# VectorE's conversion passes and scale chains: order as written, until all weights are converted

## The chip, the cores and the metric

The kernel runs on one core of a Trainium2 chip. A core has TensorE (PE, with its weight loads shown as PEld), VectorE (DVE), ScalarE (ACT), GpSimd (POOL) and SyncE (SP, which here issues the DMAs). The metric is the device time of one execution in microseconds, lower is better. Each engine takes its instructions strictly in the order of its own queue, and waits at the head of it when an input isn't there.

## The reference, cut to what matters

```python
# 8 batches, 8 heads, 512 local and 32 global tokens, head dim 64
s_ll = where(abs(i - j) <= 32, scale * q_l @ k_l.T, -1e9)      # band of 65 keys
out_l = softmax([scale * q_l @ k_g.T, s_ll]) @ [v_g, v_l]
out_g = softmax(scale * q_g @ [k_g, k_l].T) @ [v_g, v_l]
x = concat(out_g, out_l)  -> [4608, 512]
h = x @ w_in                                                   # [4608, 2048]
g = where(h > 0, h, exp(min(h, 0)) - 1)
out = g @ w_out                                                # [4608, 512]
```

The weights arrive as 64-bit floats, and are turned into 32-bit ones on the chip with integer operations.

## The kernel before, in words

**Two streams of work.** Attention goes through slots (a batch, two pairs of heads, a tile of 128 tokens): scores (L644 adds the mask and takes the row maximum, L647 scales it), the exponential on ACT (L651), the norm (L655, L656, then POOL), transposes on PE (L669), the product with v (L691), and the result into a block xr of 256 tokens with its maximum xm (L703, L705). The FFN goes through 17 such blocks; for each it multiplies by pairs of 128-column tiles of w_in (ffn1, L298), applies the ELU (ACT L307 to L309, DVE L316), and multiplies by w_out (ffn2, L373). Numbers are split in a high and a low half of 16 bits (xh and xl, gh and gl, winh and winl, wouth and woutl), and three products are summed.

**Converting the weights.** w_in and w_out come in 16 units (`unit(m, p)`, 8 pairs of each). A unit loads `raw` by DMA, and then runs in steps: s0 (ACT, then POOL L160), s1a (L164), s1b (L167) and s1c (L171), which put the bits of the 32-bit number together in `cu`, s1d (the maximum: DVE L176 for w_in, ACT for w_out), s2 (`all_max`: a PE transpose L112 and a DVE maximum L113 over all partitions, into `cm`), s3 (a chain of operations on one column, L185, L107, L187, L188, that makes the scale; then ACT L189 writes the high half) and s4 (DVE L192 writes the low half). `tables(group)` makes the scales of a group of pairs in the same way (L208 to L215, `wm_b`, `wm_c`), and POOL multiplies them into `xs` (L476 to L480).

**Splitting a block.** `split_x` does the same with a block of x: L465, `all_max`, L454, L107, L456, L457, then ACT L458 writes xh and DVE L461 writes xl.

**Groups.** While not all weights are there, a block goes through the pairs in groups a (pair 0), b (pair 1), c (2 and 3) and d (4 to 7), and its partial sums go through DRAM (`o`, L381 adds them). Once all are converted (the key "f" is in `tab`), a block goes through all eight pairs at once, with seven products of quarter blocks for eight (L413); sums of weights for that are made by `add_up` (L251 to L266).

**What sets the order.** The program writes the steps with `defer(n, fn)`: the function runs n ticks later, and a tick comes with each slot of attention or stretch of the FFN. The scheduler then sets each engine's queue by its own estimate of when operations can start, and may let an operation overtake others that were written ahead of it. `tc.keep_in_program_order(op)` adds an edge from the instruction written last ahead of `op` on its engine, which takes no semaphore and only sets order: `op` can't come ahead of that instruction. Others can still move around them. In the kernel before, two kinds of operation are held in this way: s1a (L164) and the PE transpose of `all_max` (L112).

## Time and profile before

| | us |
|---|---|
| median of 3 runs | 1017.06 |
| the runs | 1019.08, 1017.06, 1016.84 |
| the profiled execution | 1018.12 |
| its span in the trace | 1016.3 |
| PE busy in the span | 965.1 (95%) |
| DVE busy | 785.8 (77%) |
| ACT busy | 685.9 (67%) |
| POOL busy | 247.0 (24%) |

The profile is one execution. A row of the timeline has the start in microseconds from the beginning of the span, the length, the engine, the line of the kernel, the operation, and the tiles written and read; in brackets stands how long the engine was idle ahead of it, and what released it. A row of the windows has the span and each engine's busy time, then the clock that PE was granted (1.00 is full speed), the share of DMA and its GB/s. Ends of matmuls are modelled. Names in the timeline have no buffer number; where a name here has one (xm_847), it is that of the queues shown below. All 16 units are converted in the first 231 us or so.

### The profile page before, as it was taken

How to read it: one execution, taken by the hardware profiler on the slowest of the kernel's cores; microseconds unless marked ns; L12 is line 12 of the kernel's file. 1: busy time of each engine (PE TensorE's matmuls, PEld its weight loads, DVE VectorE, ACT ScalarE, POOL GpSimd, SP SyncE). 2: the span in 40 equal slices, each digit the busy share in tenths (PEclk: the TensorE clock that was granted, in tenths of full speed). 3: DMA queues.
4: the chain of work that ended last, by engine and by line, in shares of the span. 5: the costliest groups of instructions: out<-in, count | busy, mean ns of one | idle time of the engine just before them, and what ended most of it. 6: DMA issues, size and time to landing. Idle time of an engine off the chain costs nothing.

```text
span 1016.3 us, 21648 instructions
## 1 busy us (share of the span) xinstructions
PE 965.1 (95%) x8128; PEld 775.3 (76%) x8128; DVE 785.8 (77%) x2233; ACT 685.9 (67%) x1561; POOL 247.0 (24%) x442
## 2 busy tenths in 40 slices
PE   6898879989999999999999999999999999999994
PEld 4576546666667788887888888888888888888884
DVE  5789898999986778677777778787787878766663
ACT  4779868767566667676666677667666757677673
POOL 3355654234132112221212122112221211100000
PEclk9799999989999999999999999999999999999998
DMA  7535765641321113001310123012210101000000
GB/s 272 171 121 184 255 215 161 213 152 52 106 77 54 43 69 106 31 17 60 115 52 16 43 79 105 22 37 79 79 43 14 41 22 33 1 22 22 1 22 21
DMA packets 39168, 81.95 MB, mean 81 GB/s; under 512 B 3864, under 2 KB 5912, under 8 KB 39064
## 3 DMA queue, kind: packets, MB, share of 16 engines
q1 hardware_dynamic: 39064, 80.58, 23.7%
q8 instruction: 64, 1.05, 0.4%
q14 instruction: 40, 0.33, 0.1%
HBM read 65.36 MB, written 15.20 MB: 79 GB/s over the span
## 4 chain that ended last, share of the span: by engine, by line
PE 60%; DVE 21%; ACT 13%; issue 3%; POOL 1%; DMA 1%; DVEq 0%; ACTq 0%; POOLq 0%
PE h L298 20%; PE acc L413 9%; PE h L413 5%; PE pa L691 4%; PE pa L669 4%; PE pa L632 4%; ACT p L651 4%; PE pa L298 3%; DVE p L644 3%; PE pa L580 2%; DVE gl L319 2%; PE acc L373 2%; DVE g L316 2%; PE pa L413 2%; ACT g L307 2%
## 5 line engine op out<-in xcount | busy, mean ns | idle before, releaser
L298 PE MATMUL h<-xh,winh 128*128 128x256 f16 x992 | 271.4, 274 | 10.4 <-ACT xh L458 5.8
L298 PE MATMUL h<-xl,winh 128*128 128x256 f16 x992 | 271.1, 273 | 0.1
L298 PE MATMUL h<-xh,winl 128*128 128x256 f16 x992 | 271.2, 273 | 0.0
L298 PEld LDWEIGHTS <-winh 128*128 128x128 f16 x2176 | 211.6, 99 | 49.4 <-issue 20.3
L658 POOL TENSOR_SCALAR p<-p,sm 128x224 f32<-128x224 f32 x256 | 144.1, 580 | 333.5 <-DVE sm L656 191.3
L316 DVE SCALAR_TENSOR_TENSOR g<-g,hs 128x512 f32<-128x512 f32 x136 | 96.2, 707 | 96.2 <-ACT g L309 95.5
L651 ACT ACTIVATE p<-p,m 128x224 f32<-128x224 f32 x256 | 120.2, 473 | 67.1 <-DVE m L647 66.8
L413 PEld LDWEIGHTS <-gh 128*128 128x128 f16 x1456 | 141.8, 98 | 21.0 <-issue 4.8
L298 PEld LDWEIGHTS <-winl 128*128 128x128 f16 x1088 | 106.7, 98 | 13.0 <-issue 0.4
L307 ACT ACTIVATE g<-h,xs 128x512 f32<-128x512 f32 x124 | 84.9, 684 | 45.5 <-PE h L298 45.1
L338 ACT ACTIVATE gh<-gs,xs 128x640 f16<-128x640 f32 x104 | 86.4, 831 | 38.2 <-DVE gs L334 38.2
L319 DVE SCALAR_TENSOR_TENSOR gl<-gs,xs,gh 128x640 f16<-128x640 f32 x104 | 94.2, 905 | 23.1 <-ACT gh L338 22.9
L337 ACT ACTIVATE gh<-g,xs 128x256 f16<-128x256 f32 x104 | 53.3, 512 | 77.1 <-DVE g L316 77.1
L309 ACT ACTIVATE g<-g 128x512 f32<-128x512 f32 x136 | 85.8, 631 | 0.0
L308 ACT ACTIVATE hs<-h,xs 128x512 f32<-128x512 f32 x124 | 84.6, 682 | 0.0
L669 PE MATMUL pa<-ident,p 128*128 128x128 f32 x512 | 79.6, 282 | 3.4 <-POOL p L658 3.4
L413 PEld LDWEIGHTS <-gl 128*128 128x128 f16 x728 | 71.2, 98 | 12.9 <-DVE gl L319 0.5
L413 PE MATMUL acc<-raw,gh 128*128 128x256 f16 x416 | 79.4, 273 | 0.0
L319 DVE SCALAR_TENSOR_TENSOR gl<-g,xs,gh 128x256 f16<-128x256 f32 (+1 forms) x136 | 75.0, 552 | 5.3 <-ACT gh L323 5.1
L644 DVE CUSTOM_DVE_ANT_0 p<-pa,msk 128x224 f32<-128x224 f32 x228 | 76.4, 383 | 2.4 <-PE pa L632 2.2
L672 DVE COPY pt<-pa 128x512 f32<-128x512 f32 x98 | 66.6, 680 | 10.7 <-PE pa L669 10.6
L669 PEld LDWEIGHTS pa<-ident,p 128*128 128x128 f32 x512 | 61.5, 145 | 10.5 <-POOL p L658 6.2
(194 smaller groups left out, 2019.9 us busy)
## 6 DMA issues: line engine op xcount, KB each, us to landing
v<-vT SPq DMA_DIRECT2D x64, 256.0 KB, 2.7
k<-kT SPq DMA_DIRECT2D x32, 448.0 KB, 4.1
out<-o SPq DMA_DIRECT2D x34, 256.0 KB, 2.1
q<-qT SPq DMA_DIRECT2D x32, 256.0 KB, 5.4
raw<-w_in SPq DMA_DIRECT2D x8, 1024.0 KB, 6.2
raw<-w_out SPq DMA_DIRECT2D x8, 1024.0 KB, 5.2
od<-o SPq DMA_DIRECT2D x24, 256.0 KB, 2.5
o<-od SPq DMA_DIRECT2D x24, 256.0 KB, 3.1
```

Source lines behind the costliest of these rows:

```text
L298: nc.tensor.matmul(h[:, j, :], wt[:, c, f], xt[:, c, :], start=k == 0, stop=k == 11)
L307: nc.scalar.activation(g, hf, AF.Relu, scale=sc[:, p:p + 1])
L308: nc.scalar.activation(hs, hf, AF.Copy, scale=sc[:, 2 * NP + 1 + p:2 * NP + 2 + p])
L309: nc.scalar.activation(g, g, AF.Exp, scale=-1.0)
L316: nc.vector.scalar_tensor_tensor(out=g, in0=g, scalar=-1.0, in1=hs, op0=ALU.add, op1=ALU.max)
L319: nc.vector.scalar_tensor_tensor(out=dst, in0=src, scalar=sg, in1=hi, op0=ALU.mult, op1=ALU.subtract)
L338: nc.scalar.activation(gh[:, 2:7, :], s, AF.Copy, scale=sg)
L413: nc.tensor.matmul(cols, gt, w, start=first, stop=p == NP - 1 and k == len(todo) - 1)
L644: nc.vector.tensor_tensor_reduce(out=p[:, 0:KW], in0=sp[r][:, j * KW:(j + 1) * KW], in1=msk[:, mi, :], op0=ALU.add, op1=ALU.max, scale=1.0 ...
L651: nc.scalar.activation(ps[i][:, 0:KW], ps[i][:, 0:KW], AF.Exp, bias=m[:, 1, i:i + 1], scale=scale, accum_out=s[:, 0, i:i + 1])
L658: nc.gpsimd.tensor_scalar(ps[i][:, 0:KW], ps[i][:, 0:KW], s[:, 1, i:i + 1], 1.0, ALU.mult, ALU.mult)
L669: nc.tensor.transpose(tp[:, (2 * r + i) * P:(2 * r + i + 1) * P], ps[2 * j + r][:, i * P:(i + 1) * P], ident)
```

## The change

A helper `in_order(op)` calls `tc.keep_in_program_order(op)` as long as "f" isn't in `tab`; `tab` is now made further up. It is put around DVE's operations s1b, s1c, s1d (for w_in), s4, those of s3, those of the tables' last part, those of `split_x` after its first, and the maximum in `all_max` and the mask in `power`. No operation is added or taken away, and no operand changes. L185 is L192 in the kernel after the change, and so on: its lines are 7 further on from the middle of `unit` (L164 is L170, L167 is L173, L171 is L177, L176 is L182, L113 is L120, L107 is L114, L456 is L463).

```diff
@@ -101,16 +101,23 @@
     for p in ptile:
         nc.vector.memset(p[:, KW:2 * P], 0.0)

+    def in_order(op):
+
+        if "f" not in tab:
+            tc.keep_in_program_order(op)
+
+    tab = {}
+

     def power(dst, src):

-        nc.vector.tensor_scalar(dst.bitcast(I32), src.bitcast(I32), 0x7f800000, None, ALU.bitwise_and)
+        in_order(nc.vector.tensor_scalar(dst.bitcast(I32), src.bitcast(I32), 0x7f800000, None, ALU.bitwise_and))

     def all_max(dst, src):

         tp = ps_a.tile([P, 512], F32, name="pa")
         tc.keep_in_program_order(nc.tensor.transpose(tp[:, 0:P], src.to_broadcast([P, P]), ident))
-        nc.vector.tensor_reduce(out=dst, in_=tp[:, 0:P], op=ALU.max, axis=AX.X)
+        in_order(nc.vector.tensor_reduce(out=dst, in_=tp[:, 0:P], op=ALU.max, axis=AX.X))


     w1 = w_in.bitcast(I32).rearrange("(c p) (f w) -> p c f w", p=P, w=2)
@@ -126,7 +133,6 @@
     pww = wts.tile([P, NP], F32, name="pww")
     pwo = wts.tile([P, NP], F32, name="pwo")
     isc = wts.tile([P, NP], F32, name="isc")
-    tab = {}

     def load_weights(group):
         lo, hi = GROUPS[group]
@@ -164,16 +170,17 @@
                 nc.vector.tensor_scalar(ui, ui, 3, 0x3ffffff8, ALU.logical_shift_left, ALU.bitwise_and))

         def s1b():
-            nc.vector.scalar_tensor_tensor(out=ui, in0=high, scalar=-0x40000000, in1=ui,
-                                           op0=ALU.bitwise_and, op1=ALU.bitwise_or)
+            in_order(nc.vector.scalar_tensor_tensor(out=ui, in0=high, scalar=-0x40000000, in1=ui,
+                                                    op0=ALU.bitwise_and, op1=ALU.bitwise_or))

         def s1c():
-            nc.vector.scalar_tensor_tensor(out=ui, in0=low, scalar=29, in1=ui,
-                                           op0=ALU.logical_shift_right, op1=ALU.bitwise_or)
+            in_order(nc.vector.scalar_tensor_tensor(out=ui, in0=low, scalar=29, in1=ui,
+                                                    op0=ALU.logical_shift_right, op1=ALU.bitwise_or))

         def s1d():
             if m == 0:
-                nc.vector.tensor_reduce(out=mx[:, 0:1], in_=u, op=ALU.max, axis=AX.XY, apply_absolute_value=True)
+                in_order(nc.vector.tensor_reduce(out=mx[:, 0:1], in_=u, op=ALU.max, axis=AX.XY,
+                                                 apply_absolute_value=True))
             else:
                 nc.scalar.activation(low.bitcast(F32), u, AF.Abs, accum_out=mx[:, 1:2])

@@ -182,17 +189,17 @@
                 all_max(mx[:, 1:2], mx[:, 0:1])

         def s3():
-            nc.vector.tensor_scalar_max(mx[:, 1:2], mx[:, 1:2], LOW)
+            in_order(nc.vector.tensor_scalar_max(mx[:, 1:2], mx[:, 1:2], LOW))
             power(pw, mx[:, 1:2])
-            nc.vector.reciprocal(mx[:, 2:3], pw)
-            nc.vector.tensor_scalar_mul(mx[:, 3:4], mx[:, 2:3], 2.0 ** 14)
+            in_order(nc.vector.reciprocal(mx[:, 2:3], pw))
+            in_order(nc.vector.tensor_scalar_mul(mx[:, 3:4], mx[:, 2:3], 2.0 ** 14))
             nc.scalar.activation(parts[0], u, AF.Copy, scale=mx[:, 3:4])

         def s4():
-            nc.vector.scalar_tensor_tensor(out=parts[1].rearrange("p a b -> p (a b)") if m else parts[1],
-                                           in0=u.rearrange("p a b -> p (a b)") if m else u, scalar=mx[:, 3:4],
-                                           in1=parts[0].rearrange("p a b -> p (a b)") if m else parts[0],
-                                           op0=ALU.mult, op1=ALU.subtract)
+            in_order(nc.vector.scalar_tensor_tensor(out=parts[1].rearrange("p a b -> p (a b)") if m else parts[1],
+                                                    in0=u.rearrange("p a b -> p (a b)") if m else u, scalar=mx[:, 3:4],
+                                                    in1=parts[0].rearrange("p a b -> p (a b)") if m else parts[0],
+                                                    op0=ALU.mult, op1=ALU.subtract))

         d = 1 if lead[0] else 2
         lag = 7 if m else 12
@@ -210,9 +217,9 @@

         def rest():
             all_max(wm[:, 1:2], wm[:, 0:1])
-            nc.vector.reciprocal(wm[:, 2:3], wm[:, 1:2])
-            nc.vector.tensor_scalar(t[:, r], pwo[:, r], wm[:, 2:3], 8.0, ALU.mult, ALU.mult)
-            nc.vector.tensor_scalar_mul(isc[:, r], pww[:, r], -2.0 ** -28)
+            in_order(nc.vector.reciprocal(wm[:, 2:3], wm[:, 1:2]))
+            in_order(nc.vector.tensor_scalar(t[:, r], pwo[:, r], wm[:, 2:3], 8.0, ALU.mult, ALU.mult))
+            in_order(nc.vector.tensor_scalar_mul(isc[:, r], pww[:, r], -2.0 ** -28))
             tab[group] = wm[:, 1:2], t

         defer(5, rest)
@@ -451,15 +458,15 @@
                 all_max(mx[:, 1:2], mx[:, 0:1])

             def s2():
-                nc.vector.tensor_scalar_max(mx[:, 1:2], mx[:, 1:2], LOW)
+                in_order(nc.vector.tensor_scalar_max(mx[:, 1:2], mx[:, 1:2], LOW))
                 power(mx[:, 2:3], mx[:, 1:2])
-                nc.vector.reciprocal(mx[:, 3:4], mx[:, 2:3])
-                nc.vector.tensor_scalar_mul(mx[:, 4:5], mx[:, 3:4], 2.0 ** 14)
+                in_order(nc.vector.reciprocal(mx[:, 3:4], mx[:, 2:3]))
+                in_order(nc.vector.tensor_scalar_mul(mx[:, 4:5], mx[:, 3:4], 2.0 ** 14))
                 nc.scalar.activation(hf, xf, AF.Copy, scale=mx[:, 4:5])

             def s3():
-                nc.vector.scalar_tensor_tensor(out=lf, in0=xf, scalar=mx[:, 4:5], in1=hf,
-                                               op0=ALU.mult, op1=ALU.subtract)
+                in_order(nc.vector.scalar_tensor_tensor(out=lf, in0=xf, scalar=mx[:, 4:5], in1=hf,
+                                                        op0=ALU.mult, op1=ALU.subtract))
                 done.append(1)

             nc.vector.tensor_reduce(out=mx[:, 0:1], in_=mx[:, 6:10], op=ALU.max, axis=AX.X)
```

The queues differ on every engine, on DVE from about 26 to 299 us: 440 rows or so of 2233 stand elsewhere.

DVE at about 92 to 97 us: cu_1050 is a unit of w_out, winl_106 the low half of w_in, xm_847 the maxima of a block, whose scale L465 (L472 after) begins and whose transpose on PE follows. Before:

```order
L171 SCALAR_TENSOR_TENSOR cu_1050<-raw_1048,cu_1050 128x1024
L647 TENSOR_SCALAR m_1136<-m_1136 128x4
L192 SCALAR_TENSOR_TENSOR winl_106<-cu_939,cm_940,winh_105 128x4x256
L703 TENSOR_TENSOR xglob_134<-xglob_134,pa_1145 128x2x32
L705 TENSOR_REDUCE xm_847<-xr_846 128x1
L215 TENSOR_SCALAR isc_133<-pww_131 128x1
L465 TENSOR_REDUCE xm_847<-xm_847 128x1
L113 TENSOR_REDUCE xm_847<-pa_1198 128x1
```

After:

```order
L654 TENSOR_SCALAR m_1136<-m_1136 128x4
L712 TENSOR_REDUCE xm_847<-xr_846 128x1
L472 TENSOR_REDUCE xm_847<-xm_847 128x1
L199 SCALAR_TENSOR_TENSOR winl_106<-cu_939,cm_940,winh_105 128x4x256
L177 SCALAR_TENSOR_TENSOR cu_1050<-raw_1048,cu_1050 128x1024
L662 TENSOR_SCALAR sm_1137<-sm_1137 128x4
L651 ISA p0_81,m_1213<-pa_1207,msk_75 128x224
L651 ISA m_1213 128x1
L663 RECIPROCAL sm_1137<-sm_1137 128x4
L120 TENSOR_REDUCE xm_847<-pa_1198 128x1
L651 ISA p2_83,m_1213<-pa_1207,msk_75 128x224
L651 ISA m_1213 128x1
```

L171 (L177) and L192 (L199) went from ahead of L465 (L472) to behind it, and the maximum over the partitions L113 (L120) of the same block now has L644 (L651) of the next slot ahead.

DVE at about 118 to 125 us, where cm_1460 is the maximum of the w_in unit cu_1459, and o_1530 a partial sum of the output. Before:

```order
L164 TENSOR_SCALAR cu_1459<-cu_1459 128x1024
L185 TENSOR_SCALAR cm_1328<-cm_1328 128x1
L167 SCALAR_TENSOR_TENSOR cu_1459<-raw_1457,cu_1459 128x1024
L107 TENSOR_SCALAR pwo_132<-cm_1328 128x1
L319 SCALAR_TENSOR_TENSOR gl_1456<-g_1450,xs_1420,gh_1455 128x512
L187 RECIPROCAL cm_1328<-pwo_132 128x1
L171 SCALAR_TENSOR_TENSOR cu_1459<-raw_1457,cu_1459 128x1024
L188 TENSOR_SCALAR cm_1328<-cm_1328 128x1
L316 SCALAR_TENSOR_TENSOR g_1520<-g_1520,hs_1521 128x512
L176 TENSOR_REDUCE cm_1460<-cu_1459 128x1
L192 SCALAR_TENSOR_TENSOR woutl_109<-cu_1327,cm_1328,wouth_107 128x1024
L319 SCALAR_TENSOR_TENSOR gl_1526<-g_1520,xs_1489,gh_1525 128x512
```

After:

```order
L388 SCALAR_TENSOR_TENSOR o_1530<-acc_1528,xs_1341,o_1530 128x512
L192 TENSOR_SCALAR cm_1328<-cm_1328 128x1
L114 TENSOR_SCALAR pwo_132<-cm_1328 128x1
L194 RECIPROCAL cm_1328<-pwo_132 128x1
L326 SCALAR_TENSOR_TENSOR gl_1456<-g_1450,xs_1420,gh_1455 128x512
L195 TENSOR_SCALAR cm_1328<-cm_1328 128x1
L173 SCALAR_TENSOR_TENSOR cu_1459<-raw_1457,cu_1459 128x1024
L323 SCALAR_TENSOR_TENSOR g_1520<-g_1520,hs_1521 128x512
L199 SCALAR_TENSOR_TENSOR woutl_109<-cu_1327,cm_1328,wouth_107 128x1024
L177 SCALAR_TENSOR_TENSOR cu_1459<-raw_1457,cu_1459 128x1024
L326 SCALAR_TENSOR_TENSOR gl_1526<-g_1520,xs_1489,gh_1525 128x512
L182 TENSOR_REDUCE cm_1460<-cu_1459 128x1
```

L192 for woutl (L199), L319 of gl_1526 (L326) and L381 of o_1530 (L388) now stand ahead of the maximum L176 (L182), which a transpose on PE waits for.

DVE at about 148 to 153 us, where xm_1227 and xl_1732 belong to a block, mg and sg to attention's global queries, and cu_1783 and cu_1926 are units. Before:

```order
L164 TENSOR_SCALAR cu_1783<-cu_1783 128x1024
L590 TENSOR_SCALAR mg_1760<-mg_1760 128x1
L456 RECIPROCAL xm_1227<-xm_1227 128x1
L167 SCALAR_TENSOR_TENSOR cu_1783<-raw_1781,cu_1783 128x1024
L457 TENSOR_SCALAR xm_1227<-xm_1227 128x1
L598 TENSOR_TENSOR sg_1761<-sg_1761 128x1
L171 SCALAR_TENSOR_TENSOR cu_1783<-raw_1781,cu_1783 128x1024
L599 TENSOR_SCALAR sg_1761<-sg_1761 128x1
L461 SCALAR_TENSOR_TENSOR xl_1732<-xr_1226,xm_1227,xh_1731 128x1024
L600 RECIPROCAL sg_1761<-sg_1761 128x1
```

After:

```order
L461 TENSOR_SCALAR xm_1227<-xm_1227 128x1
L605 TENSOR_TENSOR sg_1761<-sg_1761 128x1
L114 TENSOR_SCALAR xm_1227<-xm_1227 128x1
L606 TENSOR_SCALAR sg_1761<-sg_1761 128x1
L463 RECIPROCAL xm_1227<-xm_1227 128x1
L607 RECIPROCAL sg_1761<-sg_1761 128x1
L182 TENSOR_REDUCE cm_1672<-cu_1671 128x1
L464 TENSOR_SCALAR xm_1227<-xm_1227 128x1
L468 SCALAR_TENSOR_TENSOR xl_1732<-xr_1226,xm_1227,xh_1731 128x1024
L120 TENSOR_REDUCE wm_c_1734<-pa_1818 128x1
L220 RECIPROCAL wm_c_1734<-wm_c_1734 128x1
L170 TENSOR_SCALAR cu_1926<-cu_1926 128x1024
```

The passes of cu_1783 went behind xl_1732, which now follows the chain's last operation L457 (L464) at once, and the maximum for the table wm_c comes right behind it.

Of the low half gl_1302, at about 108 us, L319 (L326) now stands directly behind its L316 (L323), where four short operations of cm_1171's chain stood between them before. In the same way L655 of sm_931 (L662) at about 79 us went from behind L171 and L176 of cu_939 to ahead of both.

## The prediction, made before the changed kernel was run

> **What bounds the kernel now.** I read the busy shares by stage first, then TensorE's (PE's) waits, then the groups and rows of VectorE (DVE). The windows, with span, busy time and count of PE, PEld, DVE, ACT and POOL, then the granted clock, DMA share and GB/s:
>
> ```profile
> 0.00:80.00 80.00, 67.40 (x441) 47.12 (x443) 57.11 (x253) 50.70 (x164) 31.28 (x74) 0.89 0.54 182
> 80.00:231.00 151.00, 131.41 (x916) 90.85 (x913) 136.87 (x348) 116.04 (x239) 74.79 (x102) 0.93 0.60 198
> 231.00:300.00 69.00, 67.45 (x482) 45.50 (x480) 66.87 (x132) 44.39 (x94) 22.41 (x31) 1.00 0.24 81
> 300.00:700.00 400.00, 395.98 (x3529) 329.21 (x3526) 302.02 (x914) 267.87 (x647) 80.63 (x164) 1.00 0.17 55
> ```
>
> From 300 us on PE is busy for 395.98 of 400, so PE sets the time there. From 80 to 231 us, where most weights are converted, it idles 151 − 131.41 = 19.6 us, and DVE is the fuller engine: 136.87 busy, 14.1 idle. The change reaches no further than about 299 us: the rows of DVE are the same from then on. What counts is how much earlier or later PE and DVE arrive there. PE's waits between 80 and 300 us (sum, times, longest):
>
> ```profile
> PE h L298 <- ACT xh L458: 5.8, 1, 5.8
> PE pa L112 <- DVE xm L465: 4.3, 3, 2.2
> PE pa L112 <- DVE cm L176: 2.8, 2, 2.6
> PE pa L112 <- DVE m L647: 2.0, 1, 2.0
> PE acc L373 <- DVE o L381: 1.6, 3, 0.7
> PE acc L373 <- DVE gl L319: 0.9, 1, 0.9
> PE acc L373 <- ACT gh L323: 0.8, 1, 0.8
> ```
>
> They sum to 18.2 us, nearly all behind DVE: the xh that ACT is late with waits for DVE's short chain L454 to L457. So in this stretch **DVE's position in its own queue** places PE.
>
> **The change part by part.** It adds and removes no instruction; only order moves. A pinned operation may not overtake what was written ahead of it on DVE. DVE's groups between 80 and 300 us (count, busy us, mean ns, then idle before and its releasers):
>
> ```profile
> L319 DVE SCALAR_TENSOR_TENSOR gl<-g,xs,gh 128x512 f16<-128x512 f32 x27 | 21.4, 792 | 3.1 <-ACT gh L323 2.9
> L316 DVE SCALAR_TENSOR_TENSOR g<-g,hs 128x512 f32<-128x512 f32 x28 | 20.3, 726 | 0.2 <-ACT g L309 0.2
> L171 DVE SCALAR_TENSOR_TENSOR cu<-raw,cu 128x1024 int32<-128x1024 int32 x14 | 18.6, 1331 | 0.0
> L167 DVE SCALAR_TENSOR_TENSOR cu<-raw,cu 128x1024 int32<-128x1024 int32 x13 | 16.2, 1246 | 0.0
> L644 DVE CUSTOM_DVE_ANT_0 p<-pa,msk 128x224 f32<-128x224 f32 x44 | 15.4, 379 | 0.4 <-PE pa L632 0.3 <-POOL xs L477 0.2
> L381 DVE SCALAR_TENSOR_TENSOR o<-acc,xs,o 128x512 f32<-128x512 f32 x20 | 14.8, 742 | 0.2
> L192 DVE SCALAR_TENSOR_TENSOR woutl<-cu,cm,wouth 128x1024 f16<-128x1024 f32 x7 | 9.2, 1320 | 0.7 <-ACT wouth L189 0.6
> L164 DVE TENSOR_SCALAR cu<-cu 128x1024 int32<-128x1024 int32 x13 | 9.1, 701 | 3.2 <-POOL cu L160 3.2
> L192 DVE SCALAR_TENSOR_TENSOR winl<-cu,cm,winh 128x1024 f16<-128x1024 f32 x7 | 8.9, 1277 | 1.3 <-ACT winh L189 1.2
> L176 DVE TENSOR_REDUCE cm<-cu 128x1 f32<-128x1024 f32 x7 | 8.5, 1208 | 0.0
> ```
>
> Neighbouring rows overlap by about 0.08 us, so I price a pass at its mean less 0.08: L171 1.25, L167 1.17, L176 1.13, L192 1.24 (wout) or 1.20 (win), L319 0.71, L381 0.66, L316 0.65, L164 0.62, L644 0.30. With these I count what each gate of PE gains or loses in DVE's queue. The gates (start, length, then in brackets the idle before and its releaser):
>
> ```profile
> 95.69 0.32 PE L112 MATMUL pa<-ident,xm 128*128 128x128 f32 x1 [2.22 <-DVE xm L465]
> 123.39 0.32 PE L112 MATMUL pa<-ident,cm 128*128 128x128 f32 x1 [2.60 <-DVE cm L176]
> 151.54 0.59 PE L298 MATMUL h<-xh,winh 128*128 128x256 f16 x2 [5.84 <-ACT xh L458]
> 154.90 0.27 PE L112 MATMUL pa<-ident,wm_c 128*128 128x128 f32 x1
> 162.24 0.39 PE L373 MATMUL acc<-wouth,gh 128*128 128x512 f16 x1 [0.84 <-ACT gh L323]
> 163.76 0.39 PE L373 MATMUL acc<-wouth,gl 128*128 128x512 f16 x1 [0.92 <-DVE gl L319]
> 208.64 0.29 PE L112 MATMUL pa<-ident,cm 128*128 128x128 f32 x1 [2.00 <-DVE m L647]
> 273.55 0.32 PE L112 MATMUL pa<-ident,xm 128*128 128x128 f32 x1 [1.02 <-DVE xm L465]
> 288.90 0.38 PE L373 MATMUL acc<-wouth,gh 128*128 128x512 f16 x1 [0.42 <-DVE o L381]
> ```
>
> *At 95.69 us* (xm_847) L171 and L192 go behind L465: −1.25 − 1.20 = −2.45, and the 2.22 wait goes. But four L644 and one L164 now stand ahead of the chain's end: +1.2 + 0.6 = +1.8 for its xh. *At 123.39* (cm_1460) L192, L319 and L381 come ahead of L176: 1.24 + 0.71 + 0.66 = +2.6, so the time won is waited out there. On PE some L373 matmuls move ahead of both transposes (13 before or just behind the first, six before the second); they fill the gaps with work that came later anyway, and shorten neither chain. Neither place keeps anything, because *the wait at 151.54* is 5.84 us long: PE can be later or earlier by that much ahead of it and still starts when xh comes. Ahead of that chain's last operation (L457, xm_1227) two L381 are added and L164 and L167 taken away: 1.32 − 1.79 = −0.47. *At 162 to 164* L316 and L319 (g_1837, gl_1843) lose two L171 and one L192, −3.7, so up to 0.84 + 0.92 = 1.76 of waiting goes, which PE meets again *at 208.64*: there L176 (cm_2391) has one more L316 ahead, **+0.65**. (The row names L647 as releaser; the transpose reads cm_2391, which L176 makes, so I take L176.) PE arrives there early by what it saved at 162 to 164 and waits for DVE; between 166 and 205 us its only wait is the longest of those for L381 (0.7), so it carries most of the earlier start along, and DVE alone decides when the transpose runs.
>
> So the sum is 0.65 plus the change of **DVE's idle time up to 208 us**. These rows carry the new stalls:
>
> ```profile
> 79.32 1.22 DVE L171 SCALAR_TENSOR_TENSOR cu<-raw,cu 128x1024 int32<-128x1024 int32 x1
> 80.75 0.18 ACT L651 ACTIVATION_READ_ACCUMULATOR p<-p,m 128x1 f32 x1
> 107.27 0.68 DVE L316 SCALAR_TENSOR_TENSOR g<-g,hs 128x512 f32<-128x512 f32 x1
> 108.04 0.72 ACT L323 ACTIVATE gh<-g,xs 128x512 f16<-128x512 f32 x1
> 117.67 0.69 DVE L164 TENSOR_SCALAR cu<-cu 128x1024 int32<-128x1024 int32 x1 [1.91 <-POOL cu L160]
> 150.10 0.15 DVE L457 TENSOR_SCALAR xm<-xm 128x1 f32<-128x1 f32 x1
> 151.52 1.29 DVE L461 SCALAR_TENSOR_TENSOR xl<-xr,xm,xh 128x1024 f16<-128x1024 f32 x1
> ```
>
> - L655 (sm_931) is now ahead of L171 (cu_939); its input, the last of four sums by ACT, is ready at 80.75 + 0.18 = 80.93, and DVE, which started L171 at 79.32 before, gets to it after one small L656 at about 79.5: +1.4. Behind it the whole conversion of cu_939 waits, with attention's L644.
> - L319 (gl_1302) now stands directly behind its L316, which ends at 107.95; gh is ready at 108.76: +0.8.
> - xl_1732 stands directly behind L457: 151.52 − 150.25 = +1.3, where an L171 filled the gap.
> - Behind it comes L113 of wm_c, whose transpose PE ends at 155.17; DVE is done with xl at 152.81: +2.4. Two L381 stood there, and all conversion passes are queued behind.
>
> Together +5.9. None of the four is hidden: DVE takes its queue in order, so while it waits for ACT or PE all that is written behind stands, attention's L644 and the ELU passes too, for which PE waits later. What can go: L164's two waits for POOL (the group's 3.2: the one of 1.91, and one that the wm_c stall replaces), since ACT and POOL start those units earlier against DVE; and waits of L319 and L192 for ACT, 2.9 + 1.2 + 0.6 = 4.7, where passes that now queue in order stand between. I take all of the 3.2 and half of the 4.7: −5.55. Bounds: from 0 − 7.9 to +5.9 − 0. The two ends are far apart (−7.9 and +5.9). I take 5.9 − 5.55 = **+0.35**, near the row of DVE's present idle time (14.1 us from 80 to 231): an order that opens some gaps and closes others of the same kind leaves it about there.
>
> DMA issues on SP trade places (some k loads before raw) but the DMA share is 0.60 there; their cost is taken as 0, with the 3.2 of L164 as bound, since raw feeds that pass. POOL (74.79 of 151) and ACT (116.04) get no new work.
>
> *From 231 to 300* the xm wait at 273.55 loses one 128x512 pass of add_up ahead of it (L257, priced near an L316 at 0.6) and the 0.42 at 288.90 goes, as L381 (o_3120) is about 3 us earlier: −1.0, bounds 0 to −1.44.
>
> **The clock.** Half-speed stretches follow PE's gaps:
>
> ```profile
> 96.60:100.00 3.40, 3.40 (x24) 2.42 (x23) 3.23 (x19) 2.75 (x6) 3.18 (x8) 0.50 0.84 271
> 209.20:216.00 6.80, 6.18 (x34) 4.68 (x34) 6.53 (x20) 3.37 (x11) 2.50 (x4) 0.50 0.49 154
> ```
>
> They stand behind the waits of 2.22 and 2.00 us. One such stretch with PE full costs 1.7 us, the second 3.1. I let both stay: 0, bounds −3.1 and +1.7. [...]
>
> **Sum.** +0.65 + 0.35 − 1.0 + 0 = 0.0 against the profiled run's 1018.12 us (span 1016.3 and 1.8 around it). That run lies 1.06 above the median of 1017.06, so the forecast on the median is 1017.0.
>
> **The rivals.**
> *Slower: the pinned order makes DVE wait at the head of its queue.* One mechanism: a pass that used to fill a gap may no longer jump ahead, so all four stalls above stand (+5.9) and only the 1.32 replaced by wm_c's is saved (3.2 − 1.91 = 1.3). Then 0.65 + 5.9 − 1.3 − 0.4 = +4.8: 1021.9 on the median. It decides once new idle exceeds what goes by 2.4 us. For it: 90.6% of DVE's window is busy already (136.87/151), so it can't catch up. Against: the gaps it opens are each near 1 to 2 us, and earlier waits of the same size disappear.
>
> *Faster: passes in order keep DVE fed.* The stalls don't appear, since ACT and PE run ahead of an orderly DVE; 3.2 + half of 4.7 go: 0.65 − 5.55 − 1.0 = −5.9, or 1011.2; if the half-speed stretch after 209 goes in part, 1009. For it: L316 and L319 of g_1837 and gl_1843 come 3.7 us sooner, and PE idles 19.6 us to be had. Against: the chain that feeds xh gains only 0.47.
>
> *The change does nothing* is out: some 440 lines of DVE's order differ.
>
> **How the numbers follow.** Forecast 0.37, slower rival 0.30, faster 0.33. Within 0.2% (2.0 us) is about what a measurement of this kernel can tell from no change. The forecast's own spread is 2 us, with 0.31 of its 0.37 inside 0.2% and 0.03 on either side: faster 0.36, same 0.31, slower 0.33. The range takes in both rivals: 1009 below; above, 1021.9 with one half-speed stretch more (1.7) and the profiled run's distance (1.1), 1025.
>
> **What would show it.** Right: L298 for xh near 151.5 again, the 2.22 wait gone, the cm_1460 transpose later by about 2 us, waits at 162 to 164 gone, DVE's idle in 80 to 231 near 14 us. Wrong: DVE's idle there beyond 17 us with L655, L319 and L113 as the waiting lines (slower rival), or below 11 us (faster rival). If PE reaches the first row common to both orders (L316 near 298.7 us) at another time, but the rest from 300 us takes a different time too, the reasoning that nothing changes there falls.

## The result, and the profile after

The changed kernel takes **1022.87 us** (median of 5; 1021.21 to 1024.7) against 1017.06 (median of 5; 1015.39 to 1019.08) on the same chip: a ratio of **1.0054, 95% interval 1.0038 to 1.0070**. It is slower by 5.8 us. The profiled execution took 1023.94, its span is 1022.2 against 1016.3.

The stages of the changed kernel, with the columns of the windows shown before:

```profile
0.00:80.00 80.00, 64.72 (x428) 45.15 (x429) 55.08 (x252) 49.04 (x159) 31.27 (x74) 0.87 0.54 182
80.00:231.00 151.00, 127.26 (x885) 86.94 (x884) 131.52 (x326) 111.01 (x225) 62.71 (x94) 0.93 0.56 189
231.00:300.00 69.00, 67.23 (x486) 46.13 (x485) 66.76 (x144) 46.21 (x104) 21.89 (x36) 1.00 0.29 101
300.00:700.00 400.00, 395.96 (x3515) 327.76 (x3513) 303.69 (x909) 267.32 (x642) 81.20 (x164) 1.00 0.17 55
```

DVE is busy for 131.52 of the 151 us, where it was busy for 136.87: its **idle time grew from 14.1 to 19.5 us, by 5.4**. That is about what the span grew by (5.9), but the two needn't be the same: up to 80 us DVE had already done 2.0 us less (55.08 against 57.11), and some is made up later. After 300 us the kernel is as before (PE busy for 395.96 of 400 against 395.98): a PE row that both have, L632 at 299.25 us before (L639 after), comes 5.4 us later, and the span ends 5.9 later. PE's main waits between 80 and 300 us, and below them its gates:

```profile
PE h L305 <- ACT xh L465: 9.5, 2, 7.5
PE pa L119 <- DVE cm L182: 7.7, 3, 4.9
PE acc L380 <- DVE o L388: 2.7, 2, 1.6
PE acc L380 <- ACT gh L330: 1.3, 2, 1.1
```

```profile
104.02 0.47 PE L305 MATMUL h<-xh,winh 128*128 128x256 f16 x2 [2.02 <-ACT xh L465]
129.81 0.47 PE L119 MATMUL pa<-ident,cm 128*128 128x128 f32 x1 [4.88 <-DVE cm L182]
157.73 0.59 PE L305 MATMUL h<-xh,winh 128*128 128x256 f16 x2 [7.47 <-ACT xh L465]
169.40 0.39 PE L380 MATMUL acc<-wouth,gh 128*128 128x512 f16 x1 [1.13 <-ACT gh L330]
217.28 0.44 PE L119 MATMUL pa<-ident,cm 128*128 128x128 f32 x1 [2.48 <-DVE cm L182]
```

The wait of 2.22 us for xm_847 is gone, as foreseen, and a wait of 2.02 for that block's xh has taken its place. The cm_1460 transpose comes at 129.81 instead of 123.39 (+6.4), xh of the next block at 157.73 instead of 151.54 (+6.2), the transpose of cm_2391 at 217.28 instead of 208.64 (+8.6). The loss is there by 130 us; of the 8.6 some 3 are made up by 299 us. DVE's rows at the places where it stood idle show how it came about:

```profile
82.23 0.18 DVE L662 TENSOR_SCALAR sm<-sm 128x4 f32<-128x4 f32 x1 [1.04 <-ACT p L658]
...
108.99 0.14 DVE L222 TENSOR_SCALAR isc<-pww 128x1 f32<-128x1 f32 x1
111.91 0.69 DVE L323 SCALAR_TENSOR_TENSOR g<-g,hs 128x512 f32<-128x512 f32 x1 [2.78 <-ACT g L316]
113.75 0.75 DVE L326 SCALAR_TENSOR_TENSOR gl<-g,xs,gh 128x512 f16<-128x512 f32 x1 [1.14 <-ACT gh L330]
114.42 0.69 DVE L170 TENSOR_SCALAR cu<-cu 128x1024 int32<-128x1024 int32 x1
...
157.71 1.28 DVE L468 SCALAR_TENSOR_TENSOR xl<-xr,xm,xh 128x1024 f16<-128x1024 f32 x1 [1.28 <-ACT xh L465]
161.81 0.29 DVE L120 TENSOR_REDUCE wm_c<-pa 128x1 f32<-128x128 f32 x1 [2.81 <-PE pa L119]
```

From 109.1 to 113.75 us DVE does one pass. At the head of its queue stands the ELU pass of g_1296 (L323). It waits for ACT's exponential, ACT for PE's product, PE for xh (104.02 above), and xh for a scale chain that DVE itself had run late. What stands behind, the passes of cu_1327 and cu_1459 and so the cm_1460 maximum, can't go ahead; cu_1327's first pass is one whose input was there, since POOL had ended its part at 109.9. The late xh isn't all of it. PE worked out the products behind it at half speed:

```profile
104.00:107.40 3.40, 3.38 (x17) 2.37 (x17) 3.33 (x6) 2.64 (x6) 1.84 (x2) 0.53 0.97 349
```

The 128x256 matmuls of L305 start every 0.21 us there, and every 0.11 at 1.00 (298.82 to 299.04 us). At full speed these 3.38 us would have been 1.8 (3.38 times the clock of 0.53), so by this estimate 1.6 of the 2.78 + 1.14 us that DVE idles here come from the clock. From 80 to 231 us the mean clock is the same before and after (0.93): the half-speed stretches moved (in windows of 1 us they begin at about 96.6, 123.9, 147.8 and 209.2 us before, at 104.2, 128.1, 155.4 and 216.8 after), and this one lies in the way of DVE's own next pass. DVE's longest waits from 80 to 231 us (sum, times, longest), before and after:

```profile
DVE cu L164 <- POOL cu L160: 3.2, 2, 1.9
DVE gl L319 <- ACT gh L323: 2.0, 3, 0.8
DVE cm L185 <- ACT raw L178: 1.8, 2, 1.1
DVE sm L655 <- ACT p L651: 1.5, 2, 0.9
DVE winl L192 <- ACT winh L189: 1.2, 1, 1.2
```

```profile
DVE gl L326 <- ACT gh L330: 3.7, 4, 1.4
DVE wm_c L120 <- PE pa L119: 2.8, 1, 2.8
DVE g L323 <- ACT g L316: 2.8, 1, 2.8
DVE sm L662 <- ACT p L658: 2.1, 2, 1.1
DVE woutl L199 <- ACT wouth L196: 1.7, 1, 1.7
DVE xl L468 <- ACT xh L465: 1.3, 1, 1.3
```

The waits for POOL went (3.2), and waits for PE and ACT came in their stead.

### The profile page after: what moved, and what is told of

Its sections match the earlier page's. It is cut to its first block, busy times and chain, and to the rows that moved or that the text cites. A ratio compares the mean times of both kernels' runs of the same rounds, so it can differ in the third digit from the quotient of the medians.

```text
span 1022.2 us, 21663 instructions
## 1 busy us (share of the span) xinstructions
PE 963.5 (94%) x8128; PEld 773.6 (76%) x8128; DVE 785.0 (77%) x2233; ACT 685.7 (67%) x1561; POOL 235.3 (23%) x442
## 4 chain that ended last, share of the span: by engine, by line
PE 63%; DVE 17%; ACT 13%; issue 3%; DMA 2%; POOL 1%; SPq 0%; DVEq 0%; ACTq 0%; POOLq 0%
PE h L305 22%; PE acc L420 10%; PE h L420 5%; PE pa L698 4%; PE pa L676 4%; PE pa L639 4%; ACT p L658 4%; PE acc L380 3%; PE pa L305 3%; PE pa L587 2%; PE pa L420 2%; DVE gl L326 2%; DVE p L651 2%; DVE g L323 2%; ACT g L314 2%
## 5 line engine op out<-in xcount | busy, mean ns | idle before, releaser
L305 PE MATMUL h<-xh,winh 128*128 128x256 f16 x992 | 272.3, 275 | 14.6 <-ACT xh L465 9.5
L305 PE MATMUL h<-xl,winh 128*128 128x256 f16 x992 | 272.1, 274 | 0.1
L305 PE MATMUL h<-xh,winl 128*128 128x256 f16 x992 | 272.0, 274 | 0.0
L305 PEld LDWEIGHTS <-winh 128*128 128x128 f16 x2176 | 212.5, 99 | 55.0 <-issue 25.0
L665 POOL TENSOR_SCALAR p<-p,sm 128x224 f32<-128x224 f32 x256 | 139.7, 564 | 346.2 <-DVE sm L663 183.3
L323 DVE SCALAR_TENSOR_TENSOR g<-g,hs 128x512 f32<-128x512 f32 x136 | 97.0, 713 | 99.1 <-ACT g L316 98.4
L305 PEld LDWEIGHTS <-winl 128*128 128x128 f16 x1088 | 107.0, 98 | 13.5 <-issue 0.4
L326 DVE SCALAR_TENSOR_TENSOR gl<-gs,xs,gh 128x640 f16<-128x640 f32 x104 | 94.3, 907 | 23.1 <-ACT gh L345 22.9
L316 ACT ACTIVATE g<-g 128x512 f32<-128x512 f32 x136 | 86.0, 632 | 0.0
L326 DVE SCALAR_TENSOR_TENSOR gl<-g,xs,gh 128x256 f16<-128x256 f32 (+1 forms) x136 | 74.4, 547 | 5.9 <-ACT gh L330 5.9
L651 DVE CUSTOM_DVE_ANT_0 p<-pa,msk 128x224 f32<-128x224 f32 x228 | 76.4, 386 | 3.1 <-PE pa L639 1.9
```

The source lines that it names most:

```text
L305: nc.tensor.matmul(h[:, j, :], wt[:, c, f], xt[:, c, :], start=k == 0, stop=k == 11)
L316: nc.scalar.activation(g, g, AF.Exp, scale=-1.0)
L323: nc.vector.scalar_tensor_tensor(out=g, in0=g, scalar=-1.0, in1=hs, op0=ALU.add, op1=ALU.max)
L326: nc.vector.scalar_tensor_tensor(out=dst, in0=src, scalar=sg, in1=hi, op0=ALU.mult, op1=ALU.subtract)
L651: nc.vector.tensor_tensor_reduce(out=p[:, 0:KW], in0=sp[r][:, j * KW:(j + 1) * KW], in1=msk[:, mi, :], op0=ALU.add, op1=ALU.max, scale=1.0 ...
L665: nc.gpsimd.tensor_scalar(ps[i][:, 0:KW], ps[i][:, 0:KW], s[:, 1, i:i + 1], 1.0, ALU.mult, ALU.mult)
```

## The experiments

All variants change only which operations are pinned, by the condition in `in_order` (the last one adds matmuls). An operation has a kind and a place: s1b, s1c, s1d, s3, s4 and "wmax" (the maximum in s2) with a unit (m, p); "tab" with a group; "x" (split_x's chain) and "xl" (its low half) with a block. The excerpts of code below give the condition in short; it stands in the changed kernel's `in_order` in place of the old one, so a condition that names one place leaves all others unpinned. A pin moves more than the pinned operation, since the scheduler then times everything behind it anew; the rows by which the gates move stand in the expectations. The theories: **A**, later **H**: what comes late on a short chain makes DVE idle at the head of its queue, and DVE's idle time is what is lost; **P**: the passes in strict order cost; **D**: only DVE's total idle time counts; **C**: the place of the cm_1460 maximum decides, and waits take up other delays; **S**: any other order is slower; **L**, **E**: the loss is late, or early anywhere.

**One kind of pin at a time.**

```diff
-        if "f" not in tab:
+        if kind in ("s1b", "s1c", "s1d", "s4", "xl") and "f" not in tab:     # e1
+        if kind in ("wmax", "s3", "tab", "x") and "f" not in tab:            # e2
+        if kind in ("x", "xl") and "f" not in tab:                           # e3
+        if kind != "s1b" and "f" not in tab:                                 # e4
```

> Of the pinned operations only the full-width passes stay pinned (L167, L171, L176, L192, L461); the short chains are free as before. In DVE's queue the end of block xm_847's chain then stands 0.2 us earlier than before the change, and the cm_1460 maximum 0.6 us earlier, where the change has them 2.7 and 2.5 us later. Theory A (short chains that fall behind make an ELU pass wait at the head of DVE's queue and put the loss there): within 1.5 us of the kernel before. Rival P (the passes in strict order are what costs): at least 4 us slower than before. Theory D (only DVE's total idle time counts): between, wherever its idle from 80 to 231 us goes.

Measured: 1023.28 against 1017.39, ratio 1.0051 (1.0036 to 1.0066). A foretold too little, and P's "at least 4" came true. The passes alone, with no chain late in the queue, cost as much as the whole change. DVE's waits of this kernel from 78 to 160 us are longer for POOL (3.8, where all of the window to 231 us held 3.2) and for ACT's sums, and a new one of 1.5 us stands ahead of an ELU pass:

```profile
DVE cu L172 <- POOL cu L168: 3.8, 2, 2.1
DVE sm L664 <- ACT p L660: 1.8, 2, 1.4
DVE g L325 <- ACT g L318: 1.5, 1, 1.5
```

> The reverse: only the short chains and the maxima of the transposes are pinned (L107, L113, L185 to L188, L213 to L215, L454 to L457), the full-width passes are free. The end of xm_847's chain stands 5.2 us later in DVE's queue than before, the cm_1460 maximum 1.2 us later. Theory A: 3 to 7 us slower than before, with the wait for xh at about 104 us above 3 us and an idle DVE ahead of the ELU pass of g_1296. Rival P: within 1 us of before.

Measured: 1027.24, ratio 1.0097 (1.0083 to 1.0110). Slower than the whole change, so P is out as the only cause; at 9.9 us more than before it is also 3 us beyond the top of A's range. An idle of 5.56 us stands ahead of g_1296's ELU.

> Only split_x's operations are pinned. xm_847's chain end stands 7.3 us later in DVE's queue than before; the cm_1460 maximum, xm_1227's chain and the later gates stand within 0.2 us of before. Theory A: 2 to 5 us slower, since the xh wait makes DVE idle ahead of g_1296's ELU and DVE can't catch up before cm_1460. Rival C (only the place of the cm_1460 maximum decides, since the long wait for xh at 151 us takes up earlier delays): within 1 us of before. Rival P: within 1 us.

Measured: 1029.94, ratio 1.0109 (1.0080 to 1.0137), the slowest of all, though the cm_1460 maximum stands in the queue where it did. C is out. The size is about 7 us beyond the top of A's range.

> The whole change except that L167 isn't pinned. All gates in DVE's queue stand as with the change, except that the cm_1460 maximum is 1.9 us nearer the front (0.6 us later than before, not 2.5). Theory A: the stall at 109 to 114 us is as with the change, the transpose wait of 4.88 us shrinks by about 2, but the next wait for xh grows by it, so the time is that of the change, 4.5 to 6 us slower than before. Rival C: most of the loss goes, within 2 us of before.

Measured: 1023.88, ratio 1.0055 (1.0041 to 1.0070), as A says: 1.9 us less in front of the cm_1460 maximum bring nothing.

**One place at a time, on the kernel before.**

```diff
+        if (kind, which) == ("x", 2):                                   # e5
+        if (kind, which) == ("tab", "c"):                               # e6
+        if which == (0, 2) and kind in ("s1b", "s1c", "s1d", "wmax", "s3", "s4"):   # e7
+        if (kind, which) == ("s1c", (0, 1)):                            # e8
```

> The kernel before, with the pins on the scale chain of one block only (xm_847). 42 rows of DVE's order differ, all between about 95 and 112 us; the chain's end stands 7.3 us later in DVE's queue, and from the cm_1460 maximum on all is as before. Theory H (a late scale makes DVE idle at the head of its queue, since an ELU pass waits for TensorE, which waits for xh; DVE never makes that up): DVE idles 4 to 6 us between 105 and 115 us and the time is 4 to 6 us above before. Rival C (the 2.60 us wait at 123 us and the 5.84 us wait at 151 us take up an earlier delay): within 1 us of before, with the wait at 151 us shorter by the delay.

Measured: 1023.13 against 1017.77, ratio 1.0062 (1.0043 to 1.0081). A single chain, 7.3 us late in the queue where the change has it 2.7 late, costs as much as the whole change. DVE's idle row, and PE's two waits for xh (sum, times, longest):

```profile
111.58 0.29 DVE L124 TENSOR_REDUCE cm<-pa 128x1 f32<-128x128 f32 x1 [5.53 <-PE pa L123]
```

```profile
PE h L309 <- ACT xh L469: 9.0, 2, 5.8
```

The long wait for xh is still 5.8 us: it took up nothing. This is the clearest run against the prediction's view that a delay ahead of that wait is free. PE would have had room, but the chain that PE waits for is DVE's work, and it is late by what DVE idled. In the profiles the loss can be put in its place: DVE's L655 at 86.74 us before comes 2.2 us earlier here, its L316 at 208.49 comes 4.2 later, and in between DVE lost 6.5 us. The clock has a part in it, since PE ran at half speed from 104 to 111 us:

```profile
104.00:111.00 7.00, 5.91 (x29) 4.11 (x29) 2.02 (x2) 0.00 (x0) 5.33 (x13) 0.53 0.86 293
```

At full speed these 5.91 us would have been 3.1 (5.91 times 0.53), so by this estimate up to 2.8 of DVE's 5.53 us come from the clock. No run parts the two.

> The kernel before, with the pins on the table of group c only. 118 rows differ, from about 130 us on; xm_1227's chain ends 0.5 us nearer the front, xl_1732 1.5, the ELU pass of g_1837 2.6, and two passes (L164, L167 of cu_1926) stand between xl_1732 and the maximum of wm_c. The prediction's term for the order at 150 to 164 us was a stall of +2.4 against waits of 1.3 and 1.76 that go. Theory H: no new idle of DVE above 1.5 us, time within 1.5 us of before, rather faster (-1 to -2). Rival S (any rearranged order is slower than the scheduler's own): 3 us slower or more.

Measured: 1022.14, ratio 1.0050 (1.0032 to 1.0068). A miss for H: no idle above 1.6 us, yet 4.4 us. DVE's waits from 150 to 200 us are more, and other ones (POOL 2.5 where it was 1.3; 1.5 for the DMA of a partial sum, where there was none). What comes of a new order isn't told by the gates alone.

> The kernel before, with the pins on one unit only (w_in pair 2, cu_1170). 130 rows differ, from about 104 to 160 us; the cm_1460 maximum stands 1.85 us later in the queue, xm_1227's chain 0.2 us, the cm_1927 maximum 2 us nearer the front. Theory H: +1.9 from the queue only if no stall appears; 0 to 2.5 us slower. Rival C (the place of the cm_1460 maximum decides the change's loss): 2 us slower or more, with the transpose wait at about 125 us grown to 4.5 us. Rival S: 3 us slower or more.

Measured: 1026.15, ratio 1.0068 (1.0047 to 1.0090), more than H or C foretold. The transpose at cm_1460 isn't where it goes, as C had it (PE waits there for no more than 0.5 us): DVE waits 4.36 us for POOL at 159 us.

> The kernel before, with a single pin on one pass, L171 of cu_939. 76 rows differ, from about 79 to 110 us; none of the gates looked at moves by more than 0.1 us in the queue. L655 of sm_931 now stands ahead of that L171. Theory H: DVE stalls 1.0 to 1.4 us at about 80 us for ACT's sums, TensorE's 2.22 us wait at 95.7 us grows by as much, and the time is 1 to 2.5 us above before. Rival C: within 0.7 us of before. Rival S: 3 us slower or more.

Measured: 1021.70, ratio 1.0039 (1.0027 to 1.0051). A single pin on one pass, with no gate moved, costs 3.9 us; H said 1 to 2.5.

**Controls, and the opposite.**

```diff
+        if kind in ("s4", "xl") and "f" not in tab:                     # e9
+        if which == (1, 4) and kind in ("s1b", "s1c", "s1d", "wmax", "s3", "s4"):   # e10
```
```diff
         def s1a():                                                      # e11, from before
-            tc.keep_in_program_order(
-                nc.vector.tensor_scalar(ui, ui, 3, ...))
+            op = nc.vector.tensor_scalar(ui, ui, 3, ...)
+            if (m, p) != (0, 7):
+                tc.keep_in_program_order(op)
```
```diff
+        if (kind, which) != ("tab", "c") and "f" not in tab:            # e12
```

> A control: the kernel before with pins on L192 and on split_x's L461 only. No engine's order changes by a single row. All theories: within 0.1% (1 us) of before. A difference would mean that something beside the order (names, placement, the chip) is measured, and all the other ratios would have to be read against it.

Measured: 1017.42 against 1016.75, ratio 1.0006 (0.9992 to 1.0020). Pins that move nothing cost nothing.

> The kernel before with the pins on one unit of w_out only (pair 4, cu_1783). 44 rows differ, from about 150 to 185 us; xm_1227's chain is where it was, the ELU pass of g_1837 is 1.3 us nearer the front and the cm_1927 maximum too. xl_1732 now stands behind two L381 instead of an L171, and a chain of four short operations (L185, L107, L187, L188 of cm_1672) stands together without a pass between. Theory H (what counts is DVE's idle time, place by place): DVE's idle between 150 and 200 us within 1.5 us of before's, time from -1.5 to +1.5. Rival S (any other order than the scheduler's own is slower by several us): +3 or more.

Measured: 1016.94, ratio 1.0016 (0.9998 to 1.0034). S is out: 44 rows elsewhere, and no loss that can be told.

> The opposite of the change, once: the kernel before with one pin less (L164 of the last w_in unit, cu_2390). 44 rows differ, from about 192 us on; the cm_2391 maximum stands 5.4 us nearer the front. Theory H: the 2.00 us wait of the transpose at 208.64 goes, but the L192 behind it and add_up's passes move too: -2 to +1. Rival S: +3 or more, though nothing is held in program order that wasn't before. If freeing is as slow as pinning, the pins as such are not the cause.

Measured: 1019.75, ratio 1.0031 (1.0017 to 1.0044). Slower with a pin less, so pins as such aren't the cause; but H's range was missed by 2 us. In its profile DVE's L316 at 208.49 us before comes 0.6 us earlier, as H had it, and the L316 at 231.72 comes 1.9 later: in between lies a half-speed stretch of 10.2 us, where before has 6.8.

> The changed kernel without the pins on group c's table: 46 rows differ from it, from about 150 us on. One pass (L164 of cu_1926) stands again between xl_1732 and the maximum of wm_c, but L164 and L167 of cu_1783 stand ahead of the end of xm_1227's chain, 1.8 us. Theory H: the idle of 2.81 us ahead of the maximum shrinks by 1 to 2 us and the wait for xh grows by 1.8, so the time is that of the changed kernel, +5 to +7 against before. Rival S says nothing here beyond slower than before by 3 or more.

Measured: 1025.13, ratio 1.0082 (1.0060 to 1.0105): 8.4 us, slower than the changed kernel by its median, though the intervals overlap. The wait ahead of wm_c is gone, but DVE now waits 3.74 and 1.84 us for POOL ahead of two L164, and PE waits 12.24 us for xh where it waited 7.47, far more than H's 1.8.

**Where in the program.**

```diff
+        if "b" not in tab:                                              # e13
+        if "b" in tab and "f" not in tab:                               # e14
+        if "a" not in tab:                                              # e15
+        if "b" not in tab and which not in ((0, 1), 2):                 # e16
```

> The pins of the change, but only until group b's table is written, about 107 us. DVE's order is that of the changed kernel row for row up to the ELU pass of g_1296 (row 332), then it finds back to that of before by about row 488; the cm_1460 maximum, xm_1227's chain and g_1837 stand where they did before the change, or up to 1.4 us nearer the front. Theory H (the loss is DVE's idle time, place by place): the changed kernel's extra idle up to that row (2.3 us in the first 240 rows and the 3.9 us ahead of g_1296's two passes) is all here, so 3.5 to 6 us slower than before, with an idle of 2.5 us or more ahead of g_1296. Rival L (the loss comes from the order after 115 us: the cm_1460 maximum, the stalls behind xl_1732): within 1.5 us of before.

Measured: 1024.21 against 1016.91, ratio 1.0089 (1.0071 to 1.0107). The early pins alone cost 7.3 us, more than all together and 1.3 beyond H's range; L is out. In its profile DVE idles 2.50 us ahead of a maximum that stands shortly before g_1296's ELU (for a transpose behind the late products) and 0.66 ahead of the ELU.

> The other half: the pins only from group b's table on. DVE's order is that of before up to row 335; then the cm_1460 maximum stands 1.2 us later, xl_1732 1.5 and g_1837 4.0 us nearer the front, wm_c's maximum directly behind xl_1732 as in the changed kernel. Theory H: no stall ahead of g_1296; the stalls of 1.3 and 2.8 us at xl_1732 and wm_c are here against the 1.3 and 1.2 us that go: +1 to +4. Rival L: 5 to 6 us slower, as the changed kernel.

Measured: 1020.16, ratio 1.0039 (1.0023 to 1.0055): +3.3, in H's range. With e13 that makes 10.6 where the whole change has 5.8: the parts don't add. A part of that is the clock, as the table by place below shows.

> The pins only until group a's table is written, about 44 us. 138 rows differ, all before about 90 us; all later gates stand as before to 0.1 us. Theory H: the part of the changed kernel's loss that arises before 80 us, where the prediction looked at nothing (its trace stood 1.5 to 3 us behind at 70 to 85 us): 0.5 to 2.5 us slower than before. Rival L: within 0.5 us of before.

Measured: 1016.95, ratio 1.0010 (0.9996 to 1.0025). The first stage, which the prediction left out, costs nothing that can be told by the time. It isn't quite cleared: in the profile of the changed kernel DVE's L655 at 86.74 us comes 2.6 us later, in this one 0.4.

> The pins until group b's table is written, as in the run before that cost 7.3 us, but without those of one unit (w_in pair 1, cu_939) and of one block (xm_847). The end of xm_847's chain then stands 0.2 us nearer the front than before the change, where it stood 2.7 us later; the other gates are within 0.7 us of before. 186 rows differ from before, so the order isn't the old one. Theory H (one scale that comes late, and DVE idle ahead of g_1296 because of it, carries the early loss): no idle above 1.5 us ahead of g_1296's ELU, and within 2 us of before. Rival E (the early pins cost wherever they stand): 4 us slower or more.

Measured: 1019.14 against 1017.11, ratio 1.0022 (1.0009 to 1.0036). **The early loss falls from 7.3 to 2.0 us** when that chain is on time and the unit cu_939 is unpinned too, with 186 rows still elsewhere, and DVE's wait ahead of g_1296's ELU is gone: of its waits between 95 and 110 us only one for a transpose is left.

```profile
96.32 0.29 DVE L124 TENSOR_REDUCE xm<-pa 128x1 f32<-128x128 f32 x1 [0.41 <-PE pa L123]
```

E is out. Which of the two it is, the run can't say: the chain alone cost 5.4 us in e5, one pass of cu_939 alone 3.9 in e8.

**The clock.**

```diff
     def all_max(dst, src, tag):                                         # e17, from before
         tp = ps_a.tile([P, 512], F32, name="pa")
+        if tag == "wmax:03":
+            for _ in range(6):
+                tc.keep_in_program_order(nc.tensor.matmul(tp, warm[:, 0:P], warm, start=True, stop=True))
```

> The kernel before with six more matmuls of 128x512 on TensorE, whose result nothing uses, ahead of the transpose of the cm_1460 maximum; DVE's order, ACT's, POOL's and SP's are those of before row for row. TensorE waits 2.60 us there, and runs at half speed from 123.9 to 127.3 us behind it. Clock theory: with the wait filled by 1.3 us of work, the half-speed stretch goes and the time falls by 1 to 1.7 us. Theory H (TensorE is ahead of DVE there and meets it again at the wait for xh at 151 us): whether that stretch goes or not, the xh wait changes by as much and the time stays within 0.5 us of before.

Measured: 1016.46 against 1017.11, ratio 0.9999 (0.9981 to 1.0017). The interval takes in 1.9 us less as well as 1.7 more, so the times can't tell the two theories apart. The windows around the transpose, and PE's rows:

```profile
120.50:123.90 3.40, 3.38 (x27) 2.79 (x29) 3.40 (x8) 1.55 (x3) 1.55 (x1) 1.00 0.99 334
123.90:127.30 3.40, 3.40 (x25) 2.05 (x23) 3.26 (x12) 2.75 (x8) 0.00 (x0) 1.00 0.75 246
```

```profile
120.52 0.32 PE L126 MATMUL pa<-ident,cm 128*128 128x128 f32 x1 [1.32 <-DVE cm L189]
...
146.97 0.58 PE L315 MATMUL h<-xh,winh 128*128 128x256 f16 x2 [5.85 <-ACT xh L475]
```

The wait fell from 2.60 to 1.32 us and the half-speed stretch behind it went (1.00). The wait for xh is 5.85 us as before, where H had it change. DVE's rows behind the stretch, before and in this run, show why:

```profile
127.71 0.44 DVE L588 TENSOR_REDUCE mg<-pa 128x1 f32<-128x272 f32 x1 [1.09 <-PE pa L580]
129.68 0.22 DVE L703 TENSOR_TENSOR xglob<-xglob,pa 128x64 f32<-128x64 f32 x1 [0.48 <-ACT xr L696]
```

```profile
123.50 0.43 DVE L605 TENSOR_REDUCE mg<-pa 128x1 f32<-128x272 f32 x1
125.12 0.22 DVE L720 TENSOR_TENSOR xglob<-xglob,pa 128x64 f32<-128x64 f32 x1
```

DVE waited there for products that PE ran at half speed (0.50 from 123.90 to 127.30 us of the kernel before; for the second by way of ACT), and both waits (1.09 and 0.48) are gone. With the same order DVE is 3.0 us ahead of the kernel before at 86.74 us, and 4.6 at 208.49. So in this execution the stretch was worth 1.6 us, as the clock theory said; PE's clock isn't hidden there. The time doesn't show it, since behind 209 us this execution has a half-speed stretch of 10.2 us, where before has 6.8, and loses 2.5.

**The lag by place.** DVE's rows L655 at 86.74 us, L316 at 208.49 and L316 at 231.72 of the kernel before, and by how much they come later in a run's profile; beside them the time at half speed between 200 and 235 us, from windows of 1 us:

| kernel | 86.74 | 208.49 | 231.72 | at half speed, us |
|---|---|---|---|---|
| before | 0 | 0 | 0 | 6.8 |
| e9 | -1.1 | -0.9 | -0.9 | 6.8 |
| e5 | -2.2 | +4.2 | +4.3 | 6.8 |
| e16 | +0.1 | +0.3 | -1.4 | 0 |
| e17 | -3.0 | -4.6 | -2.1 | 10.2 |
| e10 | +1.5 | +2.1 | +6.2 | 13.7 |
| e13 | +1.0 | +5.0 | +9.1 | 13.7 |
| e3 | -1.5 | +8.6 | +12.7 | 13.7 |

Between 208.49 and 231.72 us, where DVE's order is the same in all of these, the lag changes by 0 where half speed lasts 6.8 us, by 2.5 at 10.2, by 4.1 at 13.7 and by -1.6 at 0. So of e13's loss about 4 us lie ahead of 208.49, and 4.1 more in a half-speed stretch far behind its pins. Without those of the chain and of cu_939 (e16) only 0.2 of the first are left.

**DVE's idle time over all runs.** From the windows 80 to 231 us (151 less DVE's busy time), beside PE's granted clock there and the time of that profiled execution:

| kernel | DVE idle, us | clock | its time, us |
|---|---|---|---|
| e15, e16 | 12.1, 12.1 | 0.95, 0.97 | 1016.31, 1016.97 |
| before, e9 | 14.1, 14.3 | 0.93, 0.93 | 1018.12, 1017.53 |
| e8, e11 | 14.5, 15.0 | 0.93, 0.92 | 1022.08, 1019.97 |
| e17, e14 | 16.2, 16.3 | 0.93, 0.94 | 1016.09, 1019.68 |
| e10, e6 | 17.8, 18.1 | 0.91, 0.93 | 1024.88, 1023.71 |
| e1, e4 | 18.8, 18.9 | 0.92, 0.93 | 1023.78, 1021.46 |
| after, e5 | 19.5, 19.5 | 0.93, 0.91 | 1023.94, 1023.11 |
| e7, e13 | 20.6, 22.9 | 0.90, 0.88 | 1026.23, 1027.01 |
| e2, e3, e12 | 23.3, 23.4, 24.4 | 0.92, 0.90, 0.90 | 1026.82, 1031.04, 1027.57 |

Up to 16.3 us of idle time the executions took 1016.1 to 1022.1 us, from 17.8 on 1021.5 to 1031.0. Over the whole range 12 us more idle go with some 11 us more time. e8 and e17 lie off this line by 3 to 4 us. The clock goes the same way, so the table can't show that idle time alone is what is lost: a slow PE also makes DVE wait (1.09 and 0.48 us ahead of the two rows that e17 freed).

The clock of the whole execution is on record for every one. Of the kernel before, 12 executions at 0.976 took 1018.7 to 1020.3 us, and 13 at 0.980 took 1016.5 to 1018.1. Two of the changed kernel at 0.980 took 1021.2 and 1021.9. So at an equal clock the change still costs about 4 to 5 of the 5.8 us.

## Why the prediction was wrong

The time lies in the range (1009 to 1025), but the likeliest case, no change, didn't come true. The slower rival did: its 1021.9 was 1.0 below what was measured, and its chance had been put at 0.30. The prediction's own sign for it was met: DVE's idle beyond 17 us (19.5), with L655, L319 and L113 (L662, L326 and L120) among the lines that wait. That its size fits so well is in part luck: it has neither the 2.78 us ahead of g_1296 nor any half-speed stretch behind a new gap in it.

- **That DVE's position in its queue places PE** was right in the main: PE's gates came late with DVE's rows (by 6.4, 6.2 and 8.6 us). That a late PE places DVE in turn was followed at wm_c only. The waits shown as PE's sum also left out two of the view, 1.4 us for ACT's `o` and 1.2 for its `pt`.
- **The gates by work queued ahead** were right in sign where they stood alone: the 2.22 wait went, xh of xm_847 became late, the cm_1460 transpose came later. As sizes they fell short: +2.6 for cm_1460 became +6.4, since they count work and not waits.
- **"Neither place keeps anything", because the 5.84 us wait takes up what is lost ahead of it**, is the step that failed, and with it the term for **DVE's idle time, +0.35, where +5.4 was measured**. The delay sat on DVE, which makes what that wait is for; e5 shows a delay of over 5 us passing it whole, with the wait still 5.8 us, and the wait in the changed kernel grew to 7.47.
- **The stalls.** At sm_931 +1.4 were foreseen and 1.04 stood there; at xl_1732 +1.3 and 1.28; at wm_c +2.4 and 2.81; at gl_1302 +0.8 and 1.14. What wasn't foreseen is the 2.78 us ahead of g_1296's ELU, just before. The working had the late xh of that very block (+1.8) two paragraphs above, and didn't follow it through PE and ACT back to the head of DVE's queue, nor the half-speed stretch behind PE's new gap. e5 shows that such a chain can cost this much; in the changed kernel its part isn't parted from that of cu_939's pins.
- **What would go.** POOL's 3.2 went. Of the 4.7 us of waits for ACT's high halves half was taken off; they grew: L326's to 3.7 (with the 1.14 above) and L199's on woutl to 1.7 in the window. So the term taken as +0.35 was near its upper bound of +5.9.
- **The waits at 162 to 164 us**, which should go, stayed in part (1.13 and 0.18).
- **From 231 to 300 us** -1.0 was foreseen. The gap to before does shrink, from +8.6 at 208.64 to +5.4 at 299.25, but PE's waits from 231 to 300 us are 1.8 us where they were 1.4, so not by the step foreseen. The half-speed stretch behind the cm_2391 transpose was shorter in the changed kernel's profile, 3.4 us for 6.8, which is 1.7 us by estimate (half of the 3.4 less, at a clock of 0.50); the rest stays open.
- **The clock** was put at 0, by letting two stretches stay. As a sum for 80 to 231 us that held (0.93 and 0.93), but not as a reason to leave it out: here the stretches counted by where they fell. The one at 104 us lies in the way of DVE's stall (1.6 us by the estimate above); the one that e17 took away was worth 1.6 us.

What stays open: the split. e6, e7, e8 and e11 lost 1 to 6 us more than H's ranges, of which only e11's has been put in a place. And how much of the change's 5.8 us is DVE's order alone, how much PE's clock behind the new gaps, no run separates. That a late chain on DVE costs time on DVE itself is shown by e5; that DVE's idle time as a whole is the measure of the loss is only made likely by the table.

## What to carry to other kernels

On an engine that takes its queue in order, ask of each moved instruction not only how much work stands ahead of it, but what its own input waits for, and follow that round: a short chain that ends late on this engine can come back, by way of two others, as a wait at its own head (here 2.78 us ahead of an ELU pass). A long wait of another engine was no cover for a delay of the engine that it waits for: in e5 DVE idled 5.53 us, and PE's wait for xh was still 5.8 us. Look also at the granted clock right behind each new gap of PE (0.53 behind one of 2.02 us): a half-speed stretch wasn't free where another engine waited for what PE did in it (1.6 us in e17's execution). Pinning an order of short chains against long passes is worth trying only where the pinned place can be named: here one chain of six small operations, 7.3 us later in the queue, cost 5.4 us by itself. And compare two profiles by rows that both have, place by place: between 208.49 and 231.72 us, with DVE in the same order, 0 to 13.7 us at half speed went with lags of -1.6 to +4.1 us.
